# A new order for the same instructions: GpSimd's port in the planner, and a distance between operands and matmuls

## The chip, the core and the metric

One core of one Trainium2 chip runs the whole program. The metric is the device time in microseconds (us) from start to end of one execution. The engines are named PE (TensorE), ACT (ScalarE), DVE (VectorE), POOL (GpSimd) and SP (SyncE, which here only issues DMAs).

## What is computed

Attention by random features over 4 batches of 8 heads, 576 tokens and 64 channels, then two gated feed-forward layers over all 2304 tokens:

```python
def phi(x):
    proj = np.einsum('bhsd,md->bhsm', x, omega)
    h = proj - np.sum(x * x, axis=-1, keepdims=True) / 2.0
    h = h - np.max(h, axis=-1, keepdims=True)
    return np.exp(h) / np.sqrt(m)
q_p, k_p = phi(q * scale), phi(k * scale)
kv, z = np.einsum('bhsm,bhsd->bhmd', k_p, v), np.sum(k_p, axis=2)
attn = np.einsum('bhsm,bhmd->bhsd', q_p, kv) / (np.einsum('bhsm,bhm->bhs', q_p, z)[..., None] + 1e-06)
x = tokens of attn                                    # 2304 x 512
x = (silu(x @ moe_w_gate) * (x @ moe_w_val)) @ moe_w_out      # 512 -> 1536 -> 512
x = ((x @ moe2_w_a) * (x @ moe2_w_b)) @ moe2_w_out
```

## The kernel before

The tokens are cut into chunks (`spans`): 512, 512, 256, 512, 512. Chunks 0, 1 and 2 go through the two feed-forward layers one after the other (`layer(c, m)`, m the layer); the last two chunks go together through a form with seven block products instead of eight (`pair(m)`, `seven`). While one chunk is in its layers, the attention of the next is put between (`attention(c, ...)`).

The products keep float32's precision: each operand is split into a high and a low part, and three matmuls stand for one. ACT writes the high part and DVE subtracts it from the operand for the low one: for weights at L868 (ACT) and by the helper `sub` (L437, DVE), for activations in the pair by `split` (L955, ACT, and L437). In chunks 0 and 1 the weights come as 64-bit words and are decoded by two ACT operations (L847, L850) and two of DVE (L853, L856); later chunks load the decoded weights (`kept`) again, through four buffers (`r_w32`). ACT also copies results out of PSUM: L905 (an up product, with silu in layer 0), L1051 (`snap`, a first product in the pair), L932 (an output). Only when such a copy is done is its PSUM bank free for the next matmuls. ACT needs different tables for silu and for the exponentials of attention (L587); a change of table is an ACT_TABLE_LOAD. In the pair, sums and differences of activations (`combine`, L967) go to POOL or DVE.

Nothing of the order is left to the compiler. `Plan.add` records every operation with its engine, a pace and a latency, the tiles that it reads and writes, and a due time. `Plan.order` then simulates the engines with a clock of its own: at each step the engine that is free first takes, of the operations whose operands stand ready, the one with the earliest due time. The order in which operations are taken is the order of the instructions in each engine's queue, and an engine works its queue in that order. SP's DMAs are planned like the rest.

What the change touches in this planner:

- `port=True` marks an operation that needs a port which DVE and POOL share in the plan: all of POOL's `tensor_tensor`, and DVE's operations whose operands lie in SBUF. DVE's operations on PSUM have no such mark. `port[e]` is the time until which engine e holds the port. An operation that finds it held by the other is planned with the wait added to its pace; a DVE operation steps aside first, if another that needs no port is waiting. `HELD` says which share of its pace an operation holds the port, and how much less.
- `slack`: an operation counts as ready this long after its last operand, and after its buffer came free. `slack[PE]` is 0 at first; `attention` sets 4.0 (chunk 1) or 2.0 for its own operations and at its end back to 0; the pair has 0.25. A matmul that follows another on PE has none.
- `act(n)`, the planned pace of an ACT operation on n elements: 0.09 + n/1200 us from SBUF.

Of the kernel before, what the change touches and what calls it, by code (L numbers as in the profile page):

```python
# [88 lines left out]
class Plan:  # L89
# [12 lines left out]
    START = 0.7  # L102
    TABLE = 1.4
    RATE = 0.24
    HELD = {DVE: (1.0, 0.1), POOL: (0.75, 0.0)}

    def __init__(self):
        self.ops = []
# [26 lines left out]
    def order(self):  # L135
        for o in self.ops:
            o.open = len(o.deps)
            for d in o.deps:
                d.users.append(o)
            for b in o.bufs:  # L140
                b.left = b.ops
        engines = (PE, ACT, DVE, POOL, SP)
        free = dict.fromkeys(engines, self.START)
        coming = {e: [] for e in engines}
        waiting = {e: [] for e in engines}
        held = {}
        table, pipe, done = None, 0.0, []
        port = {DVE: 0.0, POOL: 0.0}

        def offer(o):  # L150

            for b in o.bufs:
                if b.slot is None:
                    r = b.ring
                    if not r.free or r.recorded[r.next] is not b:
                        held.setdefault(id(r), []).append(o)
                        return
                    r.free.sort()
                    at, b.slot = r.free.pop(0)
                    o.ready = max(o.ready, at + o.slack)  # L160
                    r.next += 1
                    again = held.pop(id(r), [])
                    for to in r.pass_on():
                        again += held.pop(id(to), [])
                    for x in again:
                        offer(x)
            heapq.heappush(coming[o.eng], (o.ready, o.n, o))

        for o in self.ops:
            if o.open == 0:  # L170
                offer(o)
        while True:
            best = None
            for e in engines:
                if waiting[e]:
                    t = free[e]
                elif coming[e]:
                    t = max(free[e], coming[e][0][0])
                else:
                    continue  # L180
                if best is None or t < best[0]:
                    best = (t, e)
            if best is None:
                break
            t, e = best
            while coming[e] and coming[e][0][0] <= t + 1e-9:
                _, _, o = heapq.heappop(coming[e])
                heapq.heappush(waiting[e], (o.due, o.n, o))
            q = waiting[e]
            _, _, o = heapq.heappop(q)  # L190
            pace, lat = o.pace, o.lat
            if o.port:
                wait = port[POOL if e == DVE else DVE] - t
                if wait > 0 and e == DVE:
                    other = [x for x in q if not x[2].port]
                    if other:
                        x = min(other)
                        q.remove(x)
                        heapq.heapify(q)
                        heapq.heappush(q, (o.due, o.n, o))  # L200
                        o = x[2]
                        pace, lat = o.pace, o.lat
                if o.port:
                    wait = max(0.0, wait)
                    share, less = self.HELD[e]
                    pace, lat = pace + wait, lat + wait
                    port[e] = t + wait + share * o.pace - less
            if o.table and o.table != table:

                other = [x for x in q if x[2].table in (None, table)]  # L210
                if table and other and o.due > t - 6.0:
                    x = min(other)
                    q.remove(x)
                    heapq.heapify(q)
                    heapq.heappush(q, (o.due, o.n, o))
                    o = x[2]
                    pace, lat = o.pace, o.lat
                else:
                    table = o.table
                    pace, lat = pace + self.TABLE, lat + self.TABLE  # L220
            o.start = t
            free[e] = t + pace
            o.end = t + lat + self.SIGNAL
            if o.size:
                pipe = max(pipe, t + 1.0) + o.size / self.RATE
                o.end = pipe + 1.2
            done.append(o)
            for u in o.users:
                u.open -= 1
                u.ready = max(u.ready, t + pace if u.eng == e == PE else o.end + u.slack)  # L230
                if u.open == 0:
                    offer(u)
            for b in o.bufs:
                b.left -= 1
                b.end = max(b.end, o.end)
                if b.left == 0 and b.ring is not None:
                    r = b.ring
                    r.free.append((b.end, b.slot))
                    again = held.pop(id(r), [])
                    for to in r.pass_on():  # L240
                        again += held.pop(id(to), [])
                    for x in again:
                        offer(x)
        if len(done) < len(self.ops):
            stuck = [o for o in self.ops if not hasattr(o, "start")]
            raise RuntimeError(f"{len(stuck)} operations wait for tiles, the first due {stuck[0].due}")
        return done
# [7 lines left out]
def attention_moe_moe(ctx: ExitStack, tc: tile.TileContext, qT, kT, q, k, v, omegaT,  # L255
# [14 lines left out]
    nc = tc.nc  # L270
# [560 lines left out]
    def weights(c, m, i, due):  # L831

        hi, lo = r_wh.buf(), r_wl.buf()
        ahead = AHEAD if c else 0.0
        parts_of[c, m, i] = (hi, lo)
        w = r_w32.buf()
        keep = i % 2
        if c <= keep:

            raw = r_w64[c == 0 and i % 4 == 3].buf()
            on(SP, dma(512), due - 14, lambda: nc.sync.dma_start(
                out=raw.tile, in_=(w1, w2)[m][i].bitcast(U32).rearrange("p (n t) -> p n t", t=2)),
               writes=[(raw, 0, 1)], after=due - EARLY)
            on(ACT, act(CW), due - ahead - 10, lambda: nc.scalar.activation(  # L847
                out=w.tile, in_=raw.tile[:, :, 1].bitcast(F32), func=AF.Abs, scale=2.0 ** -112),
                reads=[(raw, 1)], writes=[(w,)], late=LATE)
            on(ACT, act(CW), due - ahead - 10, lambda: nc.scalar.activation(  # L850
                out=raw.tile[:, :, 0], in_=raw.tile[:, :, 0], func=AF.Copy, scale=0.875 * 2.0 ** -29,
                bias=0.49), reads=[], writes=[(raw, 0)])
            on(DVE, dve(CW, True), due - ahead - 9, lambda: nc.vector.scalar_tensor_tensor(  # L853
                out=raw.tile[:, :, 0], in0=raw.tile[:, :, 1], scalar=0x80000000, in1=raw.tile[:, :, 0],
                op0=ALU.bitwise_and, op1=ALU.bitwise_or), reads=[(raw, 1)], writes=[(raw, 0)])
            on(DVE, dve(CW, True), due - ahead - 9, lambda: nc.vector.scalar_tensor_tensor(  # L856
                out=w.tile.bitcast(U32), in0=w.tile.bitcast(U32), scalar=3, in1=raw.tile[:, :, 0],
                op0=ALU.logical_shift_left, op1=ALU.bitwise_or),
                reads=[(raw, 0)], writes=[(w,)])
            if c == keep:  # L860
                d = kept[m, i] = Fixed(dram.tile([P, CW], F32, name=f"kept{m}_{i}"))
                on(SP, dma(256), due - 5, lambda: nc.sync.dma_start(out=d.tile, in_=w.tile),
                   reads=[(w,)], writes=[(d,)], late=3.0)
        else:
            d = kept[m, i]
            on(SP, dma(256), due - 14, lambda: nc.sync.dma_start(out=w.tile, in_=d.tile),
               reads=[(d,)], writes=[(w,)])
        on(ACT, act(CW), due - ahead - 7, lambda: nc.scalar.activation(  # L868
            out=hi.tile.rearrange("p a c -> p (a c)"), in_=w.tile, func=AF.Copy),
            reads=[(w,)], writes=[(hi,)])  # L870
        on(DVE, dve(CW, True), due - ahead - 6, lambda: sub(
            nc.vector, lo.tile.rearrange("p a c -> p (a c)"), w.tile,
            hi.tile.rearrange("p a c -> p (a c)")), reads=[(w,), (hi,)], writes=[(lo,)])
# [325 lines left out]
    def attention(c, u0, u1):  # L1199
# [4 lines left out]
        for p in range(NP):  # L1204
# [2 lines left out]
            if part:  # L1207
                keys(last, p, d, part * w, how)
            queries(c, p, d + part * w, (1 - part) * w, how)
        slack.update({PE: 0.0})  # L1210
        opens.update(dict.fromkeys(opens, 0.0))

    layer(0, 0)
# [52 lines left out]
```

## Time and profile before

| | us |
|---|---|
| median of 3 runs | 1028.08 (1026.17 to 1028.23) |
| the profiled execution | 1027.62 |
| its span, first to last instruction | 1025.4 |
| mean granted clock of PE | 0.996 of full speed |

The page lists busy time by engine, and the trace answers questions: idle time of an engine and which instruction ended it (its releaser), groups of instructions, instructions in order of time, and busy time in chosen stretches. The granted clock is 1.00 at 2.4 GHz and 0.50 at 1.2 GHz. A matmul of 512 columns starts some 0.23 us after the one before it and is shown with 0.39 us, since they overlap.

### The profile page before, as it was taken

To read this page: it belongs to the slowest core of one execution; us is meant where nothing else is said; L and a number is where in the kernel's file an instruction comes from. 1 tells how busy PE (TensorE), PEld (TensorE's weight loads), DVE (VectorE), ACT (ScalarE), POOL (GpSimd) and SP (SyncE) were. 2 spreads that over 40 slices of the span, in tenths; PEclk is the share of its full clock that TensorE was granted. 3 is DMA by queue.
4 is the path that set the end of the run, shared out by engine and by line. 5 is a ranking of instruction groups with operands and counts; after the bars stand their busy time and mean duration, and the time that the engine had idled before them with its cause. 6 is when DMAs were issued, how large, how long until landed. Compare 5 with 4: busy or idle time off the path is not lost. (4 is left out here: it accounts for less than half of the span.)

```text
span 1025.4 us, 15587 instructions
## 1 busy us (share of the span) xinstructions
PE 1003.3 (98%) x5212; PEld 839.6 (82%) x5212; DVE 873.1 (85%) x1697; ACT 735.8 (72%) x1519; POOL 230.1 (22%) x178
## 2 busy tenths in 40 slices
PE   7999999999999999999999999999999999999998
PEld 6878888888888878878788899888788877878886
DVE  5899899999768889899985989879799788978962
ACT  5978888897689998899868977666673645556340
POOL 1222020111203243544471234113020021302000
PEclk9999999999999999999999999999999999999999
DMA  7887786776745667556644554511212311121202
GB/s 237 252 263 251 236 262 221 231 253 208 258 154 152 201 193 240 170 161 193 194 144 135 144 165 145 165 52 52 58 37 61 93 31 42 44 61 39 62 32 83
DMA packets 92401, 153.14 MB, mean 149 GB/s; under 512 B 8736, under 2 KB 41120, under 8 KB 92320
## 3 DMA queue, kind: packets, MB, share of 16 engines
q1 hardware_dynamic: 92240, 152.11, 48.5%
q8 instruction: 41, 0.67, 0.3%
q14 instruction: 40, 0.33, 0.1%
q10 hardware_dynamic: 80, 0.03, 0.0%
HBM read 128.52 MB, written 23.59 MB: 148 GB/s over the span
## 5 line engine op out<-in xcount | busy, mean ns | idle before, releaser
L437 DVE TENSOR_TENSOR wl<-w,wh 128x512 fp32r<-128x512 f32 x256 | 191.0, 752 | 30.4 <-ACT wh L868 27.5
L887 PE MATMUL ps_m<-xh,wh 128*128 128x512 f32 (+1 forms) x504 | 189.4, 376 | 3.9 <-ACT a L905 3.2
L888 PE MATMUL ps_m<-xl,wh 128*128 128x512 f32 (+1 forms) x504 | 184.7, 366 | 0.2 <-DVE xl L437 0.2
L889 PE MATMUL ps_m<-xh,wl 128*128 128x512 f32 (+1 forms) x504 | 184.8, 367 | 0.0
L868 ACT ACTIVATE wh<-w 128x512 fp32r<-128x512 f32 x224 | 138.5, 633 | 25.1 <-DVE w L856 8.7
L437 POOL TENSOR_TENSOR rs<-xT,rs 64x576 fp32r<-64x576 f32 (+4 forms) x48 | 69.5, 1449 | 243.0 <-ACT rs L525 104.4
L887 PEld LDWEIGHTS ps_m<-xh,wh 128*128 128x128 f32 x504 | 96.2, 191 | 17.6 <-ACT a L905 3.8
L889 PEld LDWEIGHTS ps_m<-xh,wl 128*128 128x128 f32 x504 | 95.7, 190 | 15.7
L888 PEld LDWEIGHTS ps_m<-xl,wh 128*128 128x128 f32 x504 | 96.1, 191 | 11.6 <-DVE xl L437 0.8
L887 PE MATMUL ps_m<-hh,wh 128*128 128x512 f32 (+1 forms) x252 | 94.5, 375 | 0.0
L889 PE MATMUL ps_m<-hh,wl 128*128 128x512 f32 (+1 forms) x252 | 92.2, 366 | 0.0
L888 PE MATMUL ps_m<-hl,wh 128*128 128x512 f32 (+1 forms) x252 | 92.1, 365 | 0.0
L850 ACT ACTIVATE w64a<-w64a 128x512 uint32<-128x512 uint32 x90 | 60.6, 679 | 16.4 <-DMA w64a<-w 16.3
L856 DVE SCALAR_TENSOR_TENSOR w<-w,w64a 128x512 uint32<-128x512 uint32 x90 | 65.4, 729 | 1.3 <-ACT w L847 1.2
L853 DVE SCALAR_TENSOR_TENSOR w64a<-w64a 128x512 uint32<-128x512 uint32 x90 | 64.0, 717 | 2.7 <-ACT w64a L850 2.7
L847 ACT ACTIVATE w<-w64a 128x512 f32<-128x512 f32 x90 | 60.4, 677 | 0.1
L889 PEld LDWEIGHTS ps_m<-hh,wl 128*128 128x128 f32 x252 | 47.5, 189 | 8.3 <-DVE wl L437 0.3
L437 DVE TENSOR_TENSOR hl<-h,hh 128x512 fp32r<-128x512 f32 (+1 forms) x72 | 49.4, 686 | 5.7 <-ACT hh L911 5.6
L887 PEld LDWEIGHTS ps_m<-hh,wh 128*128 128x128 f32 x252 | 47.6, 189 | 6.1 <-issue 0.2
L888 PEld LDWEIGHTS ps_m<-hl,wh 128*128 128x128 f32 x252 | 47.6, 189 | 5.5
L911 ACT ACTIVATE hh<-h 128x512 fp32r<-128x512 f32 (+1 forms) x72 | 40.2, 558 | 13.1 <-DVE h L908 12.8
L908 DVE TENSOR_TENSOR h<-a,ps_m 128x512 f32<-128x512 f32 (+1 forms) x64 | 39.0, 611 | 11.6 <-PE ps_m L889 9.6
(810 smaller groups left out, 2645.0 us busy)
## 6 DMA issues: line engine op xcount, KB each, us to landing
w64a<-w SPq DMA_DIRECT2D x90, 512.0 KB, 4.2
w<-kept SPq DMA_DIRECT2D x180, 256.0 KB, 2.7
kept<-w SPq DMA_DIRECT2D x72, 256.0 KB, 4.7
w64b<-w SPq DMA_DIRECT2D x18, 512.0 KB, 4.7
kt<-k_t SPq DMA_DIRECT2D x16, 320.0 KB, 4.4
vt<-v_t SPq DMA_DIRECT2D x16, 320.0 KB, 4.3
xT<-kT SPq DMA_DIRECT2D x16, 288.0 KB, 4.1
qt<-q_t SPq DMA_DIRECT2D x16, 256.0 KB, 4.4
```

The costliest lines, as they stand in the source:

```text
L437: eng.tensor_tensor(out=out, in0=a, in1=hi.bitcast(F32), op=ALU.subtract)
L847: on(ACT, act(CW), due - ahead - 10, lambda: nc.scalar.activation(out=w.tile, in_=raw.tile[:, :, 1].bitcast(F32), func=AF.Abs, scale=2.0 * ...
L850: on(ACT, act(CW), due - ahead - 10, lambda: nc.scalar.activation(out=raw.tile[:, :, 0], in_=raw.tile[:, :, 0], func=AF.Copy, scale=0.875 ...
L853: on(DVE, dve(CW, True), due - ahead - 9, lambda: nc.vector.scalar_tensor_tensor(out=raw.tile[:, :, 0], in0=raw.tile[:, :, 1], scalar=0x80 ...
L856: on(DVE, dve(CW, True), due - ahead - 9, lambda: nc.vector.scalar_tensor_tensor(out=w.tile.bitcast(U32), in0=w.tile.bitcast(U32), scalar= ...
L868: on(ACT, act(CW), due - ahead - 7, lambda: nc.scalar.activation(out=hi.tile.rearrange("p a c -> p (a c)"), in_=w.tile, func=AF.Copy), rea ...
L887: nc.tensor.matmul(o, lhsT=hi.tile[:, wi], rhs=a, start=first, stop=False)
L888: nc.tensor.matmul(o, lhsT=hi.tile[:, wi], rhs=b, start=False, stop=False)
L889: nc.tensor.matmul(o, lhsT=lo.tile[:, wi], rhs=a, start=False, stop=last)
L908: on(DVE, dve(n), due, lambda a=a, h=h, ps=ps: nc.vector.tensor_tensor(out=h.tile[:, 0:n], in0=a.tile[:, 0:n], in1=ps[1].tile[:, 0:n], op= ...
L911: on(ACT, act(n), due + 2, lambda h=h, hh=hh: nc.scalar.activation(out=hh.tile[:, 0:n], in_=h.tile[:, 0:n], func=AF.Copy), reads=[(h,)], w ...
```

## The change

Nothing is computed in another way. Four places of the planner differ, and with them the order in the queues:

```diff
-    HELD = {DVE: (1.0, 0.1), POOL: (0.75, 0.0)}
+    HELD = {DVE: (1.0, 0.0), POOL: (0.75, 0.0)}
...
             q = waiting[e]
             _, _, o = heapq.heappop(q)
+            if e == POOL and o.port and port[DVE] > t + 1e-6:
+                heapq.heappush(q, (o.due, o.n, o))
+                free[e] = port[DVE]
+                continue
             pace, lat = o.pace, o.lat
...
-            on(ACT, act(CW), due - ahead - 10, lambda: nc.scalar.activation(
+            on(ACT, act(CW + 50), due - ahead - 10, lambda: nc.scalar.activation(
                 out=w.tile, in_=raw.tile[:, :, 1].bitcast(F32), func=AF.Abs, scale=2.0 ** -112),
                 reads=[(raw, 1)], writes=[(w,)], late=LATE)
-            on(ACT, act(CW), due - ahead - 10, lambda: nc.scalar.activation(
+            on(ACT, act(CW + 50), due - ahead - 10, lambda: nc.scalar.activation(
                 out=raw.tile[:, :, 0], in_=raw.tile[:, :, 0], func=AF.Copy, scale=0.875 * 2.0 ** -29,
...
             queries(c, p, d + part * w, (1 - part) * w, how)
-        slack.update({PE: 0.0})
+        slack.update({PE: 1.0})
```

First, when the planner comes to a POOL operation and DVE holds the port, it puts the operation back and looks at POOL again at the time when the port is free. If DVE then has another operation ready that needs the port, DVE is taken first (it stands ahead of POOL in the list of engines) and POOL is put off again. Before, POOL's operation was planned at once, with the wait added, and DVE's next one that needs the port waited for it. Second, DVE holds the port for its whole pace and not 0.1 us less. Third, the two ACT operations that decode a weight block are planned with 562 elements, where they have 512. Fourth, after the first call of `attention`, and so for `layer(0, 1)` to `layer(2, 1)`, PE's slack is 1.0 us and no longer 0; `layer(0, 0)` and the prologue come before that, and the pair sets its own.

## Rows read from the trace of the kernel before

**Rows 1.** Page, part 1: busy us, share of span, instructions of PE

```profile
PE 1003.3 (98%) x5212; PEld 839.6 (82%) x5212; DVE 873.1 (85%) x1697; ACT 735.8 (72%) x1519; POOL 230.1 (22%) x178
```

**Rows 2.** Busy time by stage: stretch, length, engines' busy us (instructions), clock, DMA share, GB/s

```profile
0.00:60.00 60.00, 52.05 (x305) 43.61 (x306) 45.72 (x135) 45.24 (x124) 12.94 (x21) 1.00 0.79 244
60.00:325.00 265.00, 265.00 (x1341) 224.11 (x1340) 235.65 (x449) 219.72 (x432) 46.21 (x31) 1.00 0.72 227
325.00:545.00 220.00, 216.78 (x1148) 176.34 (x1147) 196.56 (x399) 192.62 (x442) 96.71 (x79) 1.00 0.60 185
545.00:675.00 130.00, 125.06 (x942) 117.81 (x942) 109.45 (x208) 100.81 (x210) 35.32 (x24) 0.97 0.49 144
675.00:1025.00 350.00, 344.39 (x1484) 277.75 (x1482) 285.73 (x510) 177.39 (x315) 38.88 (x24) 1.00 0.19 54
```

**Rows 3.** PE's waits: waiting group <- releaser: us in total, times, longest

```profile
PE ps_m L887 <- ACT a L905: 3.2, 2, 2.4
PE ps_p L540 <- DVE kf L551: 2.4, 4, 0.8
```

**Rows 4.** Timeline 640 to 666.5: start, us, instruction, count [idle before <- releaser]

```profile
645.88 0.68 DVE L437 TENSOR_TENSOR wl<-w,wh 128x512 fp32r<-128x512 f32 x1
...
648.02 0.68 DVE L437 TENSOR_TENSOR xl<-ft__6280,xh 128x512 fp32r<-128x512 f32 x1
...
646.10 3.75 POOL L967 TENSOR_TENSOR xt__6097<-w64a__4843,xt__6097 128x512 f32<-128x512 f32 x1 [6.33 <-DVE ft__6361 L437]
...
649.88 0.63 ACT L955 ACTIVATE xh<-xt__6097 128x512 fp32r<-128x512 f32 x1 [3.65 <-POOL xt__6097 L967]
...
654.91 0.42 ACT L955 ACTIVATE bd__6463<-w 128x256 fp32r<-128x256 f32 x1 [1.77 <-DMA w<-kept]
...
663.81 0.51 PE L945 MATMUL ps_kv<-xh,wh 128*128 128x512 f32 x1 [2.04 <-ACT ft__6189 L1051]
```

**Rows 5.** Timeline 690 to 721, the same columns

```profile
694.42 1.29 POOL L967 TENSOR_TENSOR a__6596<-a__6596,h__6715 128x512 f32<-128x512 f32 x1
...
713.79 0.41 DVE L967 TENSOR_TENSOR qf__6465<-w,qf__6465 128x256 f32<-128x256 f32 x1
...
715.80 0.69 DVE L437 TENSOR_TENSOR hh<-h__6715,hl 128x512 fp32r<-128x512 f32 x1
...
714.01 3.62 POOL L967 TENSOR_TENSOR a__6596<-h__6715,a__6594 128x512 f32<-128x512 f32 x1 [14.51 <-DVE h__6715 L1055]
...
717.67 0.63 ACT L955 ACTIVATE hl<-a__6596 128x512 fp32r<-128x512 f32 x1 [2.64 <-POOL a__6596 L967]
...
718.84 0.50 PE L945 MATMUL ps_p<-hl,wh 128*128 128x512 f32 x1 [0.66 <-ACT w64a__5217 L1051]
719.17 0.39 PE L945 MATMUL ps_p<-hh,wh 128*128 128x512 f32 x1
```

**Rows 6.** Timeline 889 to 901, the same columns

```profile
893.95 3.69 POOL L967 TENSOR_TENSOR ft__6189<-ft__6280,h__6729 128x512 f32<-128x512 f32 x1 [14.44 <-DVE ft__6280 L1055]
...
898.84 0.50 PE L945 MATMUL ps_m<-kvs__6731,wh 128*128 128x512 f32 x1 [0.49 <-ACT raw L1051]
```

**Rows 7.** Busy time in two stretches after 663.81, columns as in rows 2

```profile
665.20:668.50 3.30, 3.30 (x10) 2.54 (x9) 2.06 (x6) 1.35 (x3) 0.00 (x0) 0.50 0.34 85
668.80:672.10 3.30, 3.30 (x16) 2.69 (x15) 1.55 (x3) 1.82 (x4) 0.00 (x0) 1.00 0.00 0
```

**Rows 8.** Groups by line: busy us, mean ns | idle before, releasers

```profile
L868 ACT ACTIVATE wh<-w 128x512 fp32r<-128x512 f32 x224 | 138.5, 633 | 25.1 <-DVE w L856 8.7 <-PE ps_m L888 6.8 <-issue 3.1
...
L847 ACT ACTIVATE w<-w64a 128x512 f32<-128x512 f32 x90 | 60.4, 677 | 0.1
```

**Rows 9.** Groups of table loads, and the timeline at 565

```profile
L905 ACT ACT_TABLE_LOAD x15 | 19.2, 1283 | 0.3
L587 ACT ACT_TABLE_LOAD x15 | 19.2, 1283 | 0.3
...
565.65 0.38 PE L887 MATMUL ps_m<-xh,wh 128*128 128x256 f32 x1 [2.43 <-ACT a L905]
```

## The prediction

> **What bounds the kernel now.** The busy shares come first: TensorE is busy 98% of the span [rows 1]. So the time is TensorE's work plus what keeps it from working, and a change of order can touch the second part only. The table by stage splits the idle time (length less PE busy) [rows 2]: 60.00 − 52.05 = 7.95 us in the prologue, 0 in 60 to 325, 3.22 in 325 to 545 (layers of chunk 1 beside the next attention), 4.94 in 545 to 675 (chunk 2 and the passage into the last pair), 5.61 in 675 to the end. Outside the prologue that is 13.8 us, and no order can gain more than this and the slow clock below; the end of the last stretch is the last results leaving and stays too.
>
> TensorE's waits [rows 3 to 6] say who ends these gaps: mostly ScalarE (copies out of PSUM at L905 and L1051 that free a bank), and VectorE at L551. GpSimd is not among them, although the change is about GpSimd. So I followed each larger wait back through the timelines of three engines.
>
> At 646 us [rows 4], GpSimd's combine at L967 begins at 646.10 and takes 3.75 us; the same form takes 1.29 with nothing in its way [rows 5]. VectorE runs operations with two operands in SBUF from 645.88 without a break until 648.02 + 0.68 = 648.70; GpSimd ends at 649.85, 1.15 us after that. So it did not get in between two of them: it began when the unbroken run of VectorE ended. ScalarE's next instruction in order is the split of this result, and ScalarE sits idle 3.65 us with weight splits queued behind it. The buffers of those weights come free late, so their loads come late (ScalarE then waits 1.77 us for one), and at 663.81 TensorE has waited 2.04 us for a copy out of PSUM at L1051.
>
> At 714 us the same [rows 5]: GpSimd ready at 714.01, VectorE unbroken from 713.79 to 715.80 + 0.69, GpSimd done after 3.62 us, ScalarE idle 2.64 us on it, the PSUM copy behind it late, TensorE idle 0.66. At 894 again [rows 6]: 3.69 us, TensorE idle 0.49.
>
> A second price hangs on long waits: after the 2.04 us wait the granted clock is 0.50 (1.2 GHz instead of 2.4) for at least 3.3 us, in which 10 matmuls run where the next 3.3 us hold 16 [rows 7]. The loss is between 3.3 × 6/16 = 1.2 (matmuls counted) and 3.3 / 2 = 1.65 (half speed throughout); I take 1.5. The waits of 0.66 and 0.49 show no such drop in their stretch.
>
> **The change part by part.** No instruction, operand or byte is added or removed; only the order on each queue moves, which the planner derives from its own clock. SP's queue is planned too: a weight load waits there for a buffer whose last reader is ScalarE or VectorE, so a split that moves on ScalarE takes its load along, past the output DMAs.
>
> (1) GpSimd gives way. Before, the planner started GpSimd's operation at once, added a wait for VectorE's current operation alone, and made VectorE's next one step aside. Rows 4 to 6 show the opposite on the chip. After, GpSimd is looked at again when VectorE's port is free, and VectorE comes first where both stand ready. So the planned end of GpSimd's combine moves behind the run, and ScalarE's queue is filled with what is ready earlier: at 646 the weight splits, at 714 and 894 the PSUM copies. What this is worth on TensorE: 2.04 + 0.66 + 0.49 = 3.2 us idle; 1.5 us of clock; and each matmul after such a wait is shown at 0.50 or 0.51 instead of 0.39 [rows 4 to 6], 3 × 0.11 = 0.3. Sum 5.0 us. In the cover: moving ScalarE's work ahead of the split costs nothing where GpSimd's result is wanted late, since that result comes at the same time as before. If TensorE wants it at once, the wait comes back under another name; its bounds are 0 and the 3.2 us above.
> For the other 150 or so GpSimd operations before 675 [rows 2] I price the new order at nothing: in 325 to 545 GpSimd is busy 96.71 of 220 us [rows 2], but not one of TensorE's longer waits ends on it [rows 3]. The bounds are a gain of the 2.4 us of waits on L551 and a loss as large.
> What does the Trainium skill say here? "SBUF — State Buffer", section "Who interferes with whom", has the pair of ports locked for a whole instruction, by whichever engine issued first, until that instruction finishes. Taken literally GpSimd would enter after one VectorE instruction; by it the new rule plans GpSimd far too late and the sum would be near 0. The timelines disagree with that reading: at 646.10 and at 714.01 GpSimd sat through the whole run.
>
> (2) HELD for VectorE from (1.0, 0.1) to (1.0, 0.0): the port is held 0.1 us longer in the plan. The new test compares exactly this time, so it belongs to (1). Alone it moves ties; I take 0, bounds ±0.5 (the 0.49 us wait is the smallest that such a shift made).
>
> (3) Decodes L847 and L850 are planned with 50 more elements, that is 50/1200 = 0.042 us each. L847 takes 677 ns, against 633 ns for the split at L868 that has the same number of elements [rows 8]: the plan gets right what was 0.04 short. The decodes run mostly in the first stretches, where TensorE's idle time is 0 between 60 and 325. Worth 0, bounds ±0.7 (one wait of the L540 or L1051 kind).
>
> (4) Slack of 1.0 us before the matmuls of layers (0,1) to (2,1), where there was none. In the plan a matmul counts as ready 1.0 us after its operands or its bank; where another matmul is ready, that one goes first, and where none is, the order stays. It covers lateness up to 1.0 us. The one large wait that it meets is at 565.65: 2.43 us on the copy L905 [rows 9]. There ScalarE is the late one, with a table load of 1.28 us just before that copy. 2.43 is more than 1.0, and other matmuls need a bank first; so I do not count it as cleared. Bounds: a gain of 2.43 and a clock drop of the size above (1.5), 3.9 us; a loss of as much, if the new order makes another such wait. The small waits on L551 belong to attention matmuls, whose slack of 2.0 or 4.0 stays.
>
> The 7.95 us of the prologue stay: the layer that starts in it has no slack yet.
>
> Against the run shown: the profiled execution took 1027.62 us (span 1025.4 and 2.2 around it), the median is 1028.08. 1028.08 − 5.0 = 1023.1.
>
> **The rivals.**
> *Larger gain (A).* Slack also opens the 565.65 wait, because something else is put between: 3.9 us more, 1019. For it: with 1.0 us more distance every chain of the layers has some reserve. Against it: the wait is 2.4 times the slack, and ScalarE is full there.
>
> *No change (B).* What the new order clears comes up elsewhere: 1028. For it: at 646 TensorE's wait comes 14 us after GpSimd's end, and other things lie between, such as ScalarE's 1.77 us on a weight load; with the three waits gone those on L551 (2.4 us in four) may grow.
> *GpSimd slips in (B2).* It would enter behind the single VectorE operation under way, 0.4 or 0.7 us, and the 3.6 to 3.7 us had another cause. Then the planner of before was right, the new one postpones results that stand ready after 1.29 + 0.69 = 2.0 us, and nothing is gained: 1028. Against it: all three ends lie 1.1 to 1.2 us behind the end of the run, which a single operation would not give. Chance 0.03. The lock rule of the Trainium skill cited above is the one that would have it so.
>
> *Slower (C).* Table loads. ScalarE swaps between exponentials and silu 30 times at 1283 ns, 15 each way [rows 9]. The planner swaps when the operation that is due first asks for the other table, and slack shifts when layers' outputs and thus their silu copies come up against attention's exponentials. One more swap there and back costs ScalarE 2.57 us; where its work stands as tight as at 565, TensorE waits 2.4 us and then runs at half clock, 3.9 us together. One such pair leaves 1.1 us of the gain of 5.0; two make it a loss: 1028.1 − 5.0 + 7.8 = 1030.9. It decides from the second extra pair in the up phases of chunks 1 and 2, of which the load before 565 is one. For it: the order of 220 us of attention is redrawn, and ScalarE is busy 192.62 there [rows 2]. Against it: a swap that falls where TensorE has work costs nothing.
>
> **How the numbers follow.** A measurement tells 0.2% (2.1 us) from no change. The forecast, 1023.1 with a range of its own of 1020.5 to 1026 (bounds of parts 2 and 3, and half of the L551 waits either way), 0.38. A, with whatever else slack clears, 1019 and below, 0.21. B and B2, 1026 to 1030, 0.15 and 0.03. C, over 1030, 0.23. Faster: 0.38 + 0.21 = 0.59 or slightly above with the best of B, 0.60; same 0.17; slower 0.23. Range: a tenth is left out on either side. Downward A and the L551 waits give 1019 − 2.4 and the remaining small waits of the pair up to 2 us more, 1014.5; upward C with a third pair, 1030.9 + 3.9 less some overlap, 1033.5.
>
> **What would show it.** GpSimd's combines in the pair may still take 3.6 us (the chip holds them as before); but no 2.6 to 3.7 us ScalarE wait on them should be left, and TensorE's waits near 663, 718 and 898 should be gone, the stretch after 665 at full clock. Slack is right if the 2.43 us wait on L905 shrinks. C shows as more than 30 table loads and new TensorE waits over 2 us with a half clock behind them. B shows as the ScalarE waits gone and PE's busy share unchanged. The prediction is wrong if new waits on ScalarE in 325 to 545 exceed the 5.0 us, or if the combines come to stand on TensorE's path by themselves.

## The result: 0.7% slower, and where the time went

The changed kernel takes 1034.46 us in the median of 4 runs (1033.73 to 1036.66), the one before 1027.81 (4 runs, 1026.17 to 1028.23). The ratio is 1.0071, interval 1.0052 to 1.0091: slower by 6.7 us, where 5.0 us less was forecast, and 1 us above the top of the range. The profiled execution took 1033.73 us, its span 1031.6. Line numbers are 4 higher than before (L551 is now L555, L967 is L971).

Page, part 1, of the kernel after, columns as in [rows 1]:

```profile
PE 1004.5 (97%) x5212; PEld 841.0 (82%) x5212; DVE 888.3 (86%) x1697; ACT 727.6 (71%) x1515; POOL 223.7 (22%) x178
```

TensorE has the same 5212 matmuls, and 1.2 us more of busy time. VectorE has the same 1697 instructions, and they take 15.2 us more; GpSimd's 178 take 6.4 us less. So VectorE takes longer over the same operands than before. That alone does not make a kernel slow: of the kernels below, the fast e10_pair01 has VectorE busy for 881.7 us and the slow e1_yield for 882.4. What counts is where the time is lost, and the next view says where. The run has two halves with a clear border, the first matmul of the last pair, at 658.83 us before and at 671.22 us after. Busy time by stage, columns as in [rows 2], first of the kernel after:

```profile
60.00:325.00 265.00, 265.00 (x1341) 224.21 (x1340) 237.93 (x445) 218.26 (x431) 41.90 (x30) 1.00 0.73 228
325.00:671.20 346.20, 331.98 (x2032) 285.12 (x2031) 305.39 (x590) 278.85 (x634) 133.40 (x104) 0.99 0.55 168
671.20:1031.60 360.40, 355.86 (x1538) 288.03 (x1536) 299.43 (x528) 184.92 (x329) 35.17 (x24) 1.00 0.19 55
```

and of the kernel before, with its own border:

```profile
325.00:658.80 333.80, 327.69 (x2034) 283.04 (x2033) 293.30 (x581) 282.44 (x632) 132.04 (x103) 0.99 0.58 174
658.80:1025.40 366.60, 358.55 (x1538) 288.86 (x1536) 298.44 (x535) 188.37 (x334) 38.88 (x24) 0.99 0.19 55
```

The last pair is shorter by 6.2 us: TensorE idles 4.5 us instead of 8.0, and its 1538 matmuls take 2.7 us less. Everything between 325 us and the pair is longer by 12.4 us: TensorE idles 14.2 us instead of 6.1, and about the same number of matmuls (2032 and 2034) takes 4.3 us more. −6.2 + 12.4 = 6.2, the difference of the two spans. So two results stand on top of each other, and the one that the prediction gave no price is the larger.

TensorE's waits, after, columns as in [rows 3]:

```profile
PE ps_p L544 <- DVE kf L555: 8.2, 4, 3.5
PE ps_p L544 <- DVE qf L555: 3.1, 2, 1.7
PE ps_m L891 <- ACT a L909: 0.7, 1, 0.7
PE ps_t L949 <- ACT ft__6155 L1055: 0.4, 1, 0.4
```

Before, beside the 2.4 us of [rows 3], on the same line:

```profile
PE ps_p L540 <- DVE qf L551: 0.2, 1, 0.2
```

So the attention's matmuls waited 2.4 + 0.2 = 2.6 us in all for VectorE's sum that frees a PSUM bank (now L555), 0.8 us at most; now it is 8.2 + 3.1 = 11.3 us, 3.5 at most. The 2.43 us wait on ScalarE's copy [rows 9] has shrunk to 0.7, and of the three waits of the pair on such copies [rows 4 to 6] one of 0.4 is left. The longest wait shows what happens. Timeline of the kernel after, 508.6 to 514.4, GpSimd's operations first, then VectorE's, then TensorE's, columns as in [rows 4]:

```profile
508.83 1.40 POOL L800 TENSOR_TENSOR qf<-qf,rec 128x512 f32<-128x512 f32 x1 [0.79 <-DVE rec L797]
510.19 1.17 POOL L783 TENSOR_TENSOR xt<-qf,fT 64x256 f32<-64x256 f32 x1
511.43 1.06 POOL L783 TENSOR_TENSOR xt<-qf,zb 64x256 f32<-64x256 f32 x1
512.58 1.37 POOL L508 TENSOR_TENSOR qt<-qt 128x512 f32<-128x512 f32 x1
...
508.67 0.66 DVE L441 TENSOR_TENSOR wl<-w,wh 128x512 fp32r<-128x512 f32 x1
509.25 1.53 DVE L441 TENSOR_TENSOR hl<-h,hh 128x512 fp32r<-128x512 f32 x1
510.70 1.21 DVE L857 SCALAR_TENSOR_TENSOR w64a<-w64a 128x512 uint32<-128x512 uint32 x1
511.83 1.21 DVE L441 TENSOR_TENSOR wl<-w,wh 128x512 fp32r<-128x512 f32 x1
512.97 1.00 DVE L513 TENSOR_SCALAR nsq<-s 128x8 f32<-128x8 f32 x1
513.88 0.74 DVE L555 TENSOR_TENSOR kf<-kf,ps_p 128x256 f32<-128x256 f32 x2
...
514.35 0.92 PE L544 MATMUL ps_p<-oms,rs 128*128 128x256 f32 x2 [3.46 <-DVE kf L555]
```

VectorE works without a break, as at 646 us [rows 4]. But GpSimd does not sit until the run ends. At 508.83 it starts inside a VectorE operation of 0.66 us and is done at 510.23; it is VectorE's next operation, the hl of L441, that takes 1.53 us instead of about 0.7. The same again at 510.19, 511.43 and 512.58: the two engines alternate, and each VectorE operation pays. The four from 509.25 take 1.53 + 1.21 + 1.21 + 1.00 = 4.95 us; with 0.68 for each of the three large ones (as L437 in [rows 4]) and 0.17 for the small L513 (it takes that with 10 elements where GpSimd is idle, at 351.09, below), it would be 2.2. So L555 starts some 2.7 us late, and TensorE waits 3.46 us for the bank. The planner had put GpSimd's operations behind the run and given VectorE the undisturbed times: in its plan L800 starts at the moment at which L555, which needs no port, begins. Held against their planned starts, VectorE's instructions are 15.0 us late at 509.25 and 17.8 us at 513.88.

```profile
351.09 0.17 DVE L513 TENSOR_SCALAR nsq<-s 128x10 f32<-128x10 f32 x1
```

A slow clock follows these waits too. Busy time in three stretches of the kernel after, behind the waits of 2.79, 1.58 and 3.46 us, the granted clock after the five engines:

```profile
357.10:360.30 3.20, 3.20 (x9) 2.51 (x8) 3.20 (x9) 2.27 (x5) 0.67 (x1) 0.50 0.55 195
445.80:449.00 3.20, 3.20 (x10) 2.45 (x9) 3.17 (x7) 0.97 (x2) 1.71 (x2) 0.50 0.00 0
514.10:517.30 3.20, 2.95 (x8) 2.42 (x9) 3.13 (x8) 0.00 (x0) 0.00 (x0) 0.50 0.16 20
```

Each holds 8 to 10 matmuls at 0.50 (1.2 GHz) where 3.3 us at the full clock held 16 in the pair [rows 7]. By the prediction's estimate of 1.5 us apiece these are 4.5 us, against one such stretch before the pair in the kernel before (behind the 2.43 us wait, 0.52 in 566.5 to 569.7): an estimated 3.0 of the 4.3 us by which about the same number of matmuls takes longer. The other 1.3 us I have not placed.

How often does GpSimd get in? Counted over both traces is every GpSimd operation that began while a VectorE operation on SBUF was under way and another one of that kind followed within 0.06 us. VectorE's reductions and reciprocals are left out: in both traces none of the 140 and the 44 took longer beside GpSimd. GpSimd got in if the next VectorE operation was stretched (by more than 0.1 us over its shortest form), and was held if that one ran at its usual length. Before: 44 cases, 35 got in, 9 were held. After: 55 cases, 49 got in, 6 were held. Where the next VectorE operation was small (2 to 10 elements per partition: L578, L582, L790, L509 of before) GpSimd got in 21 times of 21 and 25 of 25; where it had 256 elements or more, 14 of 23 and 24 of 30. No small operation followed where GpSimd worked on the pair's combines (L967 of before, L971 of after), and the three holds of the prediction are among these. But the combines are not simply held: before, GpSimd got in at 3 of 8, after at 9 of 11. In attention it got in 32 times of 36 and 40 of 44; the four holds in each kernel came before a large operation.

### The profile page after: what moved, and what is told of

It reads as the page before. It is cut to its first block, busy times and chain, and to the rows that moved or that the text cites. A ratio compares the mean times of both kernels' runs of the same rounds, so it can differ in the third digit from the quotient of the medians.

```text
span 1031.6 us, 15607 instructions
## 1 busy us (share of the span) xinstructions
PE 1004.5 (97%) x5212; PEld 841.0 (82%) x5212; DVE 888.3 (86%) x1697; ACT 727.6 (71%) x1515; POOL 223.7 (22%) x178
## 4 chain that ended last, share of the span: by engine, by line
PE 51%; DVE 6%; ACT 4%; issue 2%; DVEq 0%; ACTq 0%
PE ps_m L949 13%; PE ps_p L949 8%; PE ps_t L949 8%; PE ps_kv L949 4%; PE ps_m L892 4%; PE ps_m L891 4%; PE ps_m L893 4%; DVE wl L441 1%; PE ps_p L544 1%; ACT wh L872 1%; PE ps_t L810 1%; PE ps_kv L623 1%; DVE hl L441 1%; PE ps_kv L891 1%; PE ps_kv L892 1%
## 5 line engine op out<-in xcount | busy, mean ns | idle before, releaser
L441 DVE TENSOR_TENSOR wl<-w,wh 128x512 fp32r<-128x512 f32 x256 | 197.0, 776 | 24.6 <-ACT wh L872 21.5
L872 ACT ACTIVATE wh<-w 128x512 fp32r<-128x512 f32 x224 | 139.7, 632 | 36.2 <-DVE w L860 14.2
L441 POOL TENSOR_TENSOR rs<-xT,rs 64x576 fp32r<-64x576 f32 (+4 forms) x48 | 69.5, 1448 | 253.0 <-ACT rs L521 117.0
L891 PE MATMUL ps_m<-hh,wh 128*128 128x512 f32 (+1 forms) x240 | 91.5, 381 | 0.0
L892 PE MATMUL ps_m<-hl,wh 128*128 128x512 f32 (+1 forms) x240 | 89.2, 372 | 1.0 <-DVE hl L441 1.0
L893 PE MATMUL ps_m<-hh,wl 128*128 128x512 f32 (+1 forms) x240 | 89.0, 371 | 0.0
L860 DVE SCALAR_TENSOR_TENSOR w<-w,w64a 128x512 uint32<-128x512 uint32 x90 | 62.9, 701 | 1.7 <-ACT w L851 1.6
L441 DVE TENSOR_TENSOR hl<-h,hh 128x512 fp32r<-128x512 f32 (+1 forms) x72 | 50.3, 700 | 5.1 <-ACT hh L915 4.8
L544 PE MATMUL ps_p<-oms,rs 128*128 128x256 f32 x160 | 39.3, 306 | 11.7 <-DVE kf L555 8.2
```

The source lines that it names most:

```text
L441: eng.tensor_tensor(out=out, in0=a, in1=hi.bitcast(F32), op=ALU.subtract)
L544: on(PE, pe(0.12), d, lambda h=h, ps=ps, t=t: nc.tensor.matmul(ps.tile[:, 256 * h:256 * (h + 1)], lhsT=stacks[h].tile[:, step * t:step * t ...
L891: nc.tensor.matmul(o, lhsT=hi.tile[:, wi], rhs=a, start=first, stop=False)
L892: nc.tensor.matmul(o, lhsT=hi.tile[:, wi], rhs=b, start=False, stop=False)
L893: nc.tensor.matmul(o, lhsT=lo.tile[:, wi], rhs=a, start=False, stop=last)
```

## The experiments

The theory, once this was seen (Y): the new rule describes the last pair, not the attention phase, where GpSimd goes in behind one VectorE operation; VectorE is then later than planned, and the banks it frees with it. (That the rule describes the pair is not borne out by the count above; only the part on attention is tried here.) The rival (R): the rule is harmless, and slack, decode costs or simply another order made other work late, as any redrawn order may. For each kernel I also give three numbers from outside the medians: the start of the pair on the chip, its length, and the start that the program's own planner had worked out for the pair. The last is a planned number, not a time of the chip; the chip's start less the plan's is called the lag.

| kernel | us | ratio (interval) | pair starts | pair takes | planned start | lag |
|---|---|---|---|---|---|---|
| before | 1027.81 | | 658.8 | 366.6 | 651.5 | 7.3 |
| after | 1034.46 | 1.0071 (1.0052–1.0091) | 671.2 | 360.4 | 648.9 | 22.3 |
| e1_yield | 1033.64 | 1.0064 (1.0047–1.0080) | 670.9 | 360.7 | 650.3 | 20.6 |
| e2_slack | 1022.94 | 0.9968 (0.9958–0.9979) | 659.4 | 361.7 | 651.8 | 7.6 |
| e3_decode | 1021.81 | 0.9950 (0.9935–0.9965) | 657.0 | 362.3 | 649.4 | 7.6 |
| e5_noyield | 1022.41 | 0.9955 (0.9940–0.9970) | 659.2 | 361.9 | 651.9 | 7.3 |
| e6_after_01 | 1026.61 | 0.9995 (0.9985–1.0005) | 664.6 | 361.2 | 654.8 | 9.8 |
| e7_pair | 1028.60 | 1.0015 (1.0005–1.0025) | 669.1 | 360.4 | 656.2 | 12.9 |
| e8_after_short | 1016.16 | 0.9887 (0.9867–0.9907) | 654.5 | 360.4 | 648.9 | 5.6 |
| e9_before_short | 1022.09 | 0.9945 (0.9925–0.9964) | 656.6 | 364.1 | 651.5 | 5.1 |
| e10_pair01 | 1020.29 | 0.9946 (0.9934–0.9957) | 657.4 | 360.5 | 649.4 | 8.0 |
| e11_held | 1021.18 | 0.9955 (0.9938–0.9972) | 657.8 | 360.9 | 651.9 | 5.9 |
| e12_slack09 | 1034.33 | 1.0081 (1.0060–1.0102) | 671.6 | 360.4 | 648.8 | 22.8 |
| e13_attn | 1033.62 | 1.0076 (1.0055–1.0097) | 669.7 | 360.8 | 652.9 | 16.8 |
| e14_small | 1030.90 | 1.0034 (1.0022–1.0047) | 668.2 | 360.4 | 653.0 | 15.1 |

Ratios stand against the runs of the kernel before that were taken beside each kernel (medians 1026.04 to 1027.81).

The lag can be followed along the run, by VectorE's instructions against their planned starts. At 325 us it is 0.1 us before and 0.0 after, at 545 us 5.8 and 19.2. Over the same stage it grows from 0.9 to 18.7 in e1_yield, from −0.2 to 5.9 in e10_pair01 and from −0.3 to 4.8 in e8_after_short. So most of the lag of the slow kernel arises in 325 to 545, in the layers that run beside attention.

### The parts one at a time

e1_yield is the kernel before with parts (1) and (2) alone:

```
-    HELD = {DVE: (1.0, 0.1), POOL: (0.75, 0.0)}
+    HELD = {DVE: (1.0, 0.0), POOL: (0.75, 0.0)}
...
+            if e == POOL and o.port and port[DVE] > t + 1e-6:
+                heapq.heappush(q, (o.due, o.n, o))
+                free[e] = port[DVE]
+                continue
```

> Only parts 1 and 2 (GpSimd yields in the plan, HELD 0.0); no slack, decodes planned as before. Theory Y (the planner that makes GpSimd yield counts on a VectorE that nothing holds up; the chip lets GpSimd in and the L551 adds come late): TensorE's waits on L551 in 325 to 545 us are over 6 us with at least two half-clock stretches behind them, time 1031 to 1037 us. Theory S (the slack did it): the three waits behind GpSimd's combines are gone and nothing new appears, 1021 to 1025 us. Theory R (any new order redraws the waits): between 1024 and 1034 us, with large waits at other places than in the changed kernel.

Measured 1033.64, in Y's range and at the upper end of R's; but R wanted the large waits elsewhere, and they are of the same kind as after (with one stretch at half clock, where Y expected two or more), which the waits of TensorE show:

```profile
PE ps_p L544 <- DVE kf L555: 8.2, 7, 3.4
```

e2_slack has part (4) alone, e3_decode part (3) alone, e5_noyield both:

```
-        slack.update({PE: 0.0})
+        slack.update({PE: 1.0})
...
-            on(ACT, act(CW), due - ahead - 10, ...
+            on(ACT, act(CW + 50), due - ahead - 10, ...
```

> Only part 4 (slack 1.0 us before the layers' matmuls). Theory Y: about the time of before, 1024 to 1030 us, and the waits of ScalarE on GpSimd's combines (2.6 to 3.7 us at 646, 714, 894) are still there. Theory S: 1032 to 1040 us with waits over 6 us on L551. Theory R: anything from 1024 to 1034 us.

> Only part 3 (two decode operations planned 0.042 us longer). Theories Y and S: no effect, within 2 us of before. Theory R: even this moves the time by 2 to 6 us either way, because the order in 325 to 545 us is drawn anew.

> The changed kernel without parts 1 and 2 (slack and decode only). Theory Y: the loss is gone, 1023 to 1030 us, waits on L551 at most 3 us. Theory S: the loss stays, 1032 us or more. Theory R: 1024 to 1034 us.

Measured 1022.94, 1021.81 and 1022.41: none of the three is slower, each is faster by 0.3 to 0.5%. The loss belongs to parts (1) and (2), as Y had it, but each time lies below Y's range, and in e5_noyield the waits on L551 are 4.3 us where Y allowed 3; what R expected of e3_decode, 2 to 6 us either way, came true. The three gain mostly in the pair (4.3 to 4.9 us each), where none of them touches the rule for GpSimd. A small change of due times was enough to remove the largest of the three waits there, the 2.04 us; in each of the three kernels TensorE still waits 0.6 and 0.4 to 0.5 us on copies of L1051, and ScalarE up to 2.6 us on a combine.

e11_held has part (2) alone, the constant without the rule.

> Only part 2 (HELD for VectorE 0.0 instead of 0.1), nobody yields. Theory Y1: a small step in the plan that draws a new order, within 5 us of before, first matmul of the pair 656 to 662 us. Rival (the 0.1 us is itself the harm): 1031 us or more.

Measured 1021.18: the constant alone is not the cause; it gains 4.9 us, by a pair that is 5.7 us shorter. So it is the rule in (1), together with the constant that it compares.

### The rule made inert, and the rule in one place only

e6_after_01 is the kernel after with HELD as it was, so that in the plan the port seems free 0.1 us before VectorE's operation ends and GpSimd goes in behind one operation:

```
-    HELD = {DVE: (1.0, 0.0), POOL: (0.75, 0.0)}
+    HELD = {DVE: (1.0, 0.1), POOL: (0.75, 0.0)}
```

> The changed kernel with HELD for VectorE put back to (1.0, 0.1), all else as changed. In the plan GpSimd is then looked at 0.1 us before VectorE is free, and so goes in behind the one VectorE operation under way instead of behind the whole run. Theory Y1 (the loss is the assumption that a run of VectorE keeps GpSimd out to its end; where GpSimd arrives during one VectorE operation, the traces mostly show it going in behind that one): the loss is gone, 1020 to 1027 us, waits on L551 at most 4.5 us. Theory Y2 (it is the postponing as such): 1030 us or more.

Measured 1026.61. The same four parts without the effect of the rule: 7.9 us less than after, the lag 9.8 instead of 22.3. The bank waits on kf are 4.6 us in all, a little over the 4.5 expected.

e7_pair and e10_pair01 give way only for the combines of the pair (L967 of before), elsewhere GpSimd enters as before; both have part (3) and no slack. e7_pair has HELD at 0.0, e10_pair01 at 0.1:

```
-        ... combine planned with port=True
+        ... combine planned with port=2
-            if e == POOL and o.port and port[DVE] > t + 1e-6:
+            if e == POOL and o.port == 2 and port[DVE] > t + 1e-6:
                 heapq.heappush(q, (o.due, o.n, o))
-                free[e] = port[DVE]
+                free[e] = port[DVE] + self.HELD[DVE][1]     # e10 only
```

> Decodes planned 0.042 us longer, and GpSimd yields in the plan (HELD 0.0) only for the sums and differences L967 of the pair, not for attention; no slack. Theory Y1: the order up to 545 us is nearly that of the decode change alone, so no L551 waits over 2 us; ScalarE's waits of 2.4 to 2.6 us on GpSimd in the pair that stood in the decode change alone are gone, and TensorE's 0.4 to 0.6 us behind them: 1019 to 1021.5 us against 1021.8 for the decode change. Rival (the HELD of 0.0 does the harm in attention by itself): 1028 us or more.

> Decodes planned 0.042 us longer, HELD as before (1.0, 0.1), and GpSimd yields to a run of VectorE only for L967, the sums and differences of the pair. Theory Y1 (yielding harms where GpSimd and VectorE alternate, in attention, and helps where VectorE runs unbroken, in the pair): the layers end as in the decode change alone (first matmul of the pair near 657 us), and the pair takes 360.4 us as in the changed kernel instead of 362.3: 1019 to 1021 us, the fastest so far. Rival (the pair's gain is a redraw too): 1021 to 1026 us, pair over 361.5 us.

e7_pair came out at 1028.60, 7 us more than expected and in the range of its rival: its pair is as short as hoped (360.4), but the layers are late already in the plan (656.2 instead of 651.5) and 12.9 us later than that on the chip, with a wait of 2.6 us on the bank although GpSimd does not give way in attention. So this run speaks for R, or for the HELD of 0.0; e11_held, with that constant alone, is not slow. e7_pair's trace has 34 table loads where before has 30 [rows 9]; I did not test whether they are the cause. e10_pair01 gives 1020.29, the lowest median of the kernels here that compute everything (e11_held has 1021.18), and less than both given ones. The two differ by 0.1 us in one constant, which e10_pair01 adds again where a combine is put off, and by 8.3 us in time. First pair matmul and waits of e10_pair01:

```profile
657.38 0.39 PE L952 MATMUL ps_m<-kt__4409,wh 128*128 128x512 f32 x1
...
PE ps_p L547 <- DVE kf L558: 1.5, 4, 0.7
```

e13_attn is the counterpart: the rule everywhere but for the combines.

```
-            if e == POOL and o.port == 2 and port[DVE] > t + 1e-6:
+            if e == POOL and o.port is True and port[DVE] > t + 1e-6:
```

> Decodes planned 0.042 us longer, HELD 0.0, and GpSimd yields everywhere but for L967, the sums and differences of the pair: the other half of the part tried for the pair alone. Theory Y1: the loss of the layers' part alone, first matmul of the pair at 667 to 673 us, pair 361.5 to 363 us, 1031 to 1037 us. Theory R: 1020 to 1029 us.

Measured 1033.62: the loss is here, in the layers and their attention, with another plan than after (no slack). Not all of it stands at the bank: TensorE waits 6.2 + 1.3 us on VectorE's sum, and 5.1 us on ScalarE's copy L912 (L905 of before, 3.7 us there). The pair takes 360.8 us without the rule, less than the 361.5 to 363 expected.

e12_slack09 is the kernel after with slack 0.9 instead of 1.0.

> The changed kernel with a slack of 0.9 instead of 1.0 us: the same yielding, another order. Theory Y1: the loss is there again, first matmul of the pair at 667 us or later, 1030 to 1038 us. Theory R (an unlucky draw): 1020 to 1028 us.

Measured 1034.33. Its order is nearly that of after, so this says only that the time belongs to the order and not to a single unlucky execution.

### The collision itself

This is the run that tells Y from R without a new order. e8_after_short keeps every queue of the kernel after as it is and lets GpSimd's attention operations work on every fourth column; e9_before_short does the same to the kernel before.

```
-                nc.gpsimd.tensor_tensor(out=x, in0=x, in1=x, op=ALU.mult)
+                nc.gpsimd.tensor_tensor(out=x[:, ::4], in0=x[:, ::4], in1=x[:, ::4], op=ALU.mult)
...
-                nc.gpsimd, rs.tile[other, 0:width], rT.tile[own_, 0:width],
-                rs.tile[own_, 0:width]), ...
+                nc.gpsimd, rs.tile[other, 0:width:4], rT.tile[own_, 0:width:4],
+                rs.tile[own_, 0:width:4]), ...
...
-                out=f.tile[:, g:g + 2], in0=f.tile[:, g:g + 2], ...
+                out=f.tile[:, g:g + 2, :, ::4], in0=f.tile[:, g:g + 2, :, ::4], ...
```

> The changed kernel's order, but GpSimd's operations of attention (squares, sums of L779 and L796's kind, low parts) work on every fourth column only; this leaves out three quarters of that work. If the waits on L551 come from GpSimd holding VectorE up between its operations: the waits on L551 in 325 to 545 us fall from 11 us to under 3 us, no half clock there, 1018 to 1026 us. If they come from ScalarE (exponentials, table loads) or from TensorE's own order: they stay over 6 us, 1030 us or more.

> The same shortening in the order of before, as a control; this leaves out three quarters of GpSimd's work in attention. If the order of before already has GpSimd's share planned in, little is left to gain: 1 to 5 us, 1022 to 1027 us. If the shortening gives as much here as in the changed order (8 us or more), it is not the order that makes the difference.

Measured 1016.16 and 1022.09, the second as expected. Shorter GpSimd operations save 18.3 us in the order of after (1034.46 − 1016.16) and 4.5 to 5.7 us in that of before (against the 1026.56 beside it, or 1027.81). In after's order they give back the loss of the layers and more: the pair starts at 654.5 instead of 671.2, the lag is 5.6 instead of 22.3. The stage 325 to 545 of e8_after_short and its waits:

```profile
325.00:545.00 220.00, 216.90 (x1147) 177.54 (x1146) 178.37 (x405) 191.25 (x444) 51.70 (x79) 0.99 0.58 182
...
PE ps_p L551 <- DVE kf L562: 2.3, 3, 1.8
```

GpSimd is still busy 51.70 us there, but L562 (L555 of after) now costs TensorE 2.3 us in three waits. One of them, 1.8 us, still has a half clock behind it, which the expectation had excluded, and the time lies 2 us below its range. VectorE takes 178.37 us for 405 instructions where before it took 196.56 for 399 [rows 2]. Against R: no instruction moved on a queue, only the length of GpSimd's operations. What the run does not part: shorter operations also make GpSimd's own results ready earlier. And the planned order of after is by itself a good one (planned start 648.9, the earliest with e12_slack09's); the chip does not keep to it.

e14_small goes after the reason: it is the kernel after, except that the planner lets a ready GpSimd operation go ahead of a small VectorE one (under 0.15 us), which is what the chip did in 46 of 46 cases.

```
+            if e == DVE and o.port and o.pace < 0.15 and free[POOL] <= t + 1e-6:
...
+                if waiting[POOL] and waiting[POOL][0][2].port:
+                    heapq.heappush(q, (o.due, o.n, o))
+                    e, q = POOL, waiting[POOL]
+                    _, _, o = heapq.heappop(q)
```

> The changed kernel, but in the plan GpSimd goes in ahead of VectorE's smallest operations (4 to 32 elements, planned under 0.15 us: scale, maximum plus norm, bias, denominator) instead of behind them; behind all others it yields as changed. Theory Y3 (in attention the runs that the plan assumed are broken by these small operations, where the traces show GpSimd going in every time): most of the loss of 7.5 us is gone, 1022 to 1029 us, waits on L551 in total at most 5 us, the pair still at 360 to 361.5 us. Rival (GpSimd also goes in between large operations, and that is what costs): 1030 us or more, with L551 waits over 6 us.

Measured 1030.90, in the range of the rival and not of Y3: half of the loss is back (3.6 of 6.7 us), and half is not. Its waits of TensorE on the sum that frees the bank:

```profile
PE ps_p L552 <- DVE kf L563: 5.2, 4, 2.4
PE ps_p L552 <- DVE qf L563: 2.4, 2, 1.3
```

7.6 us instead of 11.3. The lag falls from 22.3 to 15.1, but the plan itself grows by 4.1 us. At 545 us VectorE's lag is 8.9 us, where it is 19.2 after and 5.8 before; so in the stage beside attention this plan is closer to the chip, and what is lost is lost in the plan and after 545. That GpSimd goes ahead of small operations explains a part at most; a new order alone can be worth as much (parts 2 to 4 above), so this run does not prove even that part. Open stays what decides before large VectorE operations, where GpSimd got in 38 times of 53 and was held 15 times; I found nothing that sorts these cases.

## Why the prediction was wrong

*What bounds the kernel.* Right: the time is TensorE's work and what keeps it from working, and the difference is made of idle time (+8.1 and −3.5 us) and of matmuls that take longer or less long, half clock included (+4.3 and −2.7 us).

*Part (1), the three chains of the pair: right in size, the mechanism not shown.* Of the 5.0 us forecast, 3.2 were idle time; measured in the pair are 3.5 us less idle and 2.7 us less busy time, 6.2. But the sign that the prediction named for its mechanism, no wait of 2.6 us or more left to ScalarE on the combines, is not there: ScalarE still waits up to 2.8 us (3.65 before [rows 4]), and behind it TensorE waits 0.4 us at most. Waits of ScalarE on L971, after:

```profile
ACT hh L959 <- POOL xt__6001 L971: 2.8, 1, 2.8
ACT kf__5360 L959 <- POOL xt__6001 L971: 2.5, 1, 2.5
ACT hh L959 <- POOL a__6597 L971: 1.5, 1, 1.5
```

In e2_slack, e3_decode, e5_noyield and e11_held, all without the rule, the pair takes 360.9 to 362.3 us as well. The 2.04 us wait of before, the largest, was a coincidence of one order that every redrawn order here loses. With the rule for the combines the pair takes 360.4 to 360.7, and 360.8 in e13_attn without it, so the rule can claim 0.1 to 1.9 us beside that. This part of the gain was luck in its size.

*Part (1), the other 150 GpSimd operations: this step failed.* I priced the new order there at nothing, with bounds of 2.4 us either way, because none of TensorE's longer waits ended on GpSimd or, but for 2.4 us, on VectorE [rows 3]. The stage from 325 us to the pair grew by 12.4 us; with parts (1) and (2) alone, in e1_yield, the pair starts 12 us later than before. VectorE came late at the PSUM banks, and the waits on them grew from 2.6 to 11.3 us. The failure has two halves. First, the three timelines on which I took it as a fact that GpSimd waits for the end of VectorE's run had been found by following TensorE's waits back. They were a choice by consequence: cases with a bad end. Counted over the whole trace before, GpSimd was held in 9 of 44 cases, and 35 show it entering behind one operation, as the old planner had it. Second, small waits under an order that fits the chip are no bound for an order that does not. The right question would have been what L551 costs if VectorE comes late by what one entry costs it (0.5 to 0.9 us each in the four at 509 to 513), several times in a row.

The Trainium skill, "SBUF — State Buffer", section "Who interferes with whom", which I set aside on three rows, has the pair of ports locked for one whole instruction, whichever engine issues first, while the other is blocked. Read as in the prediction, with GpSimd entering behind one VectorE instruction, the traces agree in 35 of 44 cases before and 49 of 55 after, and disagree in the rest, those at 646, 714 and 894 us among them. Rival B2, built on it with a chance of 0.03, named the right mechanism for the attention phase, though it forecast no loss.

*Part (2), HELD: too narrow.* Priced at 0 ± 0.5; alone it gains 4.9 us against the runs beside it (1026.04). *Part (3), decodes: too narrow.* Priced at 0 ± 0.7; alone it gains 4.2 us (against 1026.06). *Part (4), slack.* Priced at 0 ± 3.9; alone it gains 3.1 us (against 1026.06), inside. Its own test, that the 2.43 us wait on L905 shrinks, holds in after (0.7 at most on L909, L905 of before) and with slack alone (e2_slack, 1.9). But it holds in e3_decode too (0.8), without slack, so the test did not single slack out. For parts (2) and (3) the bounds were sized from single waits. But each redraws the order of the last pair too, where some 5 us stood ready to be won by a redrawing. The gains don't add: parts (3) and (4) together (e5_noyield) give 3.7 us, between the two.

*Rival C, slower by table loads: right in sign, wrong in mechanism.* There are fewer loads. Groups of table loads, after:

```profile
L909 ACT ACT_TABLE_LOAD x13 | 16.7, 1283 | 0.2
L591 ACT ACT_TABLE_LOAD x13 | 16.7, 1283 | 0.4 <-DVE bias L586 0.2
```

26 instead of 30 [rows 9], and TensorE's longest wait on ScalarE before the pair is 0.7 us. New long waits with a half clock behind them came as C had it (1.58, 2.79 and 3.46 us), but behind VectorE. The sentence on what would make the prediction wrong looked for new waits on ScalarE in 325 to 545; the stretch was right and the engine was not.

So Y holds for attention, within limits: the five kernels that give way in the attention phase take 1030.9 to 1034.5 us and lag their plan by 15 to 23 us, the others (but for the two with shortened work) 1020.3 to 1028.6 with lags of 6 to 13, and taking three quarters of GpSimd's attention work away in the same order takes the loss away. R is right beside it: a redrawn order alone moves the time by 3 to 8 us, and e7_pair lags by 12.9 us with no rule in attention. That spread bounds how finely the loss can be put down to one rule.

## What to carry over

A rule for who goes first at a shared port is to be counted over every meeting of the two engines in the trace, with the phases kept apart, before a planner is built on it; three cases found by following the worst waits back are chosen for their bad end, and say nothing of how often it comes. For a planner, compare the time it plans with the time the chip gives at a few landmarks: here a lag that grew from 7 to 22 us said that the model had got worse although the plan had got better. And where a kernel's order is derived, any edit redraws it; its price has bounds as wide as the largest coincidences of the order before, here some 5 us, even if the edit itself is worth 0.04 us.

## What the runs showed of the hardware

- GpSimd, starting while a VectorE operation on SBUF ran, went in ahead of the next one in 46 of 46 cases where that had 2 to 10 elements per partition, and in 38 of 53 where it had 256 or more (both traces). The VectorE operation that is passed pays: 0.17 us became 1.00 (L513), 0.68 became 1.21 to 1.53. VectorE's reductions (140 in each trace, 0.65 to 0.69 us where they read 512 elements) and reciprocals (44, at most 0.18 us) never paid.
- Over the three long held runs GpSimd takes 3.62 to 3.75 us instead of 1.29 [rows 4 to 6]; in the four operations at 508.83 to 512.58, where the two alternate, it takes 1.06 to 1.40 and VectorE takes the loss. What decides between the two is open.
- The granted clock fell to 0.50 behind TensorE waits of 1.58, 2.79 and 3.46 us, in the three stretches shown, and did not after waits of 1.48 and 1.65 us (497 and 589 us, matmuls of 512 columns still 0.39 to 0.40 us and of 256 columns 0.28). So the length of a wait alone does not say whether the slow clock follows.
